# Attention with a learned position bias and a mixture-of-experts layer: half of the last 64 queries' bias transfers issued by GpSimd, bias blocks in alternating order, first tokens split later, later tiles' tokens turned between weights

## The chip, the cores and the metric

The kernel runs on one core of a Trainium2 chip. The metric is the device time of one execution in microseconds (us), as the median of the runs. Engines: TensorE (PE in the profile; PEld is its weight load), VectorE (DVE), ScalarE (ACT), GpSimd (POOL) and SyncE (SP), which here only issues transfers. "L414" is line 414 of the kernel before.

## What is computed

```
scores = q @ k^T / 8                      # 8 batches, 8 heads, 576 queries, head size 64
x      = log1p(|i - j|) / log1p(max(i, 1))
bias   = relu(x * w1 + b1) @ w2           # 32 hidden units, one bias per head, query and key
attn   = softmax(scores + bias) @ v       # the same bias table for all batches
tokens = attn, 4608 rows of 512
logits = tokens @ w_gate + modality_bias  # 8 experts
e      = argmax(logits);  g = softmax(logits)[e]
out    = g * (relu(tokens @ w1[e]) @ w2[e])   # 1024 hidden units
```

## The kernel before

**Bias table.** The table is computed once and stays in SBUF: NBm for the first 512 queries, NBr for the last 64. `bias_table` goes through 32 blocks of 16 queries by 8 heads. `bias_hidden` (L180) computes the 32 hidden units for four queries at a time, four times per block: one of the four on ScalarE (L189), three on VectorE (L191). `bias_out` (L194) multiplies by w2 on TensorE, `bias_put` (L208) scales the result out of PSUM into one of eight rotating buffers, and SyncE issues the transfer of the buffer into the table. Block `blk` of the 32 goes to every eighth partition of NBm from `blk % 8` on (L218). The query rows of NBr come in four late blocks, 32 to 35 (`bias_late`, L260); each of these is moved by four smaller transfers into every eighth partition of one half of NBr (L223, `par` picks the half).

**Attention.** Pairs of heads, 32 of them, run as a pipeline of five steps per pair (`ORDER`), one step for each 128 queries and a last one for the remaining 64 queries of both heads. The string gives the order in which each step's operations are written to the engines: S is scores on TensorE (L400) and the sum with the bias and row minimum on VectorE (L414), e and f the exponentials on ScalarE, t and T the transposes of the result, a, A, b and c the products with v (L486), C a small copy on GpSimd (L434), 0 and 1 the split of the next pair's q and k into a high and a low part (ScalarE casts the high part; GpSimd subtracts for the low part, L384). The late bias blocks are hung into the first pair's steps (`LATE`): blocks 32 and 33 are written ahead of step 0, blocks 34 and 35 ahead of step 1. Only the fifth step of a pair (c = 4) reads NBr. The engines work through their own queues in order, so what is written first is done first on each.

**Experts.** After a batch's attention, routing steps rank its tokens and GpSimd scatters the rows by expert into a DRAM table xg (`s_send`, L857 to L868). Then 18 tiles of 256 tokens of one expert each follow. A tile (`tile`) has phase 1 (96 products with w1, L1212), with the splits of the tile's w2 beside it, and phase 2 (48 products with w2, L1229), with the splits of the next tile's w1 beside it: for each weight part, ScalarE casts the high part and VectorE subtracts for the low part (`wsplit`, L1173 and L1174). The tokens of the next tile are prepared by `xprep`: GpSimd copies gates and ids, VectorE turns the tokens (L1194), ScalarE casts the high part (L1195), VectorE subtracts the low part (L1196). `put_rows` scales a result on ScalarE (L1237) and GpSimd scatters it to the output (L1238).

The first five tiles take tokens of the first six batches, so they run while the last batch is still being routed. `moe_first` hands out those routing steps by a string, one entry per call of `beside` (six per tile; X is a step of the chain with the five `s_send`, B one of the other chain). `first_tiles` hangs the preparation of the first tile into the last five attention steps: `xprep(0)` ahead of step 0, the split of the first w1 columns (`wsplit_cols(0)`, L1181 and L1182) ahead of step 3. A read of xg waits for the writes of xg that are written before it, and the other way round.

Of the kernel before, what the change touches and what calls it, by code (L numbers as in the profile page):

```python
# [22 lines left out]
S = 576  # L23
# [85 lines left out]
class Attn:  # L109
# [8 lines left out]

    ON_POOL, ON_DVE = (), (1,)


    LAG = 1
    PUT_DVE, ON_ACT2 = (21, 31, 34), ()
    TURN0, SPLIT0, QK1 = (4, 8), (6, 10), (9, 10, 11, 12, 13, 14, 15, 16)
    V0 = (0, 1)
    ROUTE = (6, 7, 8, 15, 16, 18)

    ROUTE_LATE = ((1, 1), (1, 2), (1, 3), (1, 4), (2, 0), (2, 1), (2, 3), (3, 0), (3, 1))  # L130

    LATE_HIDDEN = ((31, 0),)
    LATE = ((0, 1), (0, 0), (0, 2), (0, 1), (0, 3), (1, 2), (1, 3))

    def bias_setup(self):
# [72 lines left out]
    def bias_put(self, blk, parts):  # L208
        nc = self.nc
        o = next(self.bias_outs)  # L210
        for cols, ps in parts:
            if blk in self.PUT_DVE:
                nc.vector.tensor_scalar_mul(o[:, cols], ps, self.rpsi[:, blk : blk + 1])
            else:
                nc.scalar.activation(o[:, cols], ps, AF.Copy, scale=self.rpsi[:, blk : blk + 1])
        if blk < NMAIN:
            c, k = divmod(blk, GS)
            nc.sync.dma_start(self.NBm[k:P:GS, H * c : H * c + H, :], o)  # L218
        else:
            for par in range(2):  # L220
                for a in range(2):
                    r = 64 * par + 2 * (blk - NMAIN) + a
                    nc.sync.dma_start(self.NBr[r : 64 * par + 64 : GS, :, :], o[64 * a + par : 64 * a + 64 : 2, :])  # L223

    def bias_table(self, hooks):

        ready = {}
        self.late = [self.bias_late(blk) for blk in range(NMAIN, NBLK)]

        def ahead(blk, cg):  # L230
            if blk < NMAIN and (blk, cg) not in ready:
                by = "pool" if cg == 3 and blk in self.ON_POOL else "act" if cg == 0 and blk not in self.ON_DVE or cg == 1 and blk in self.ON_ACT2 else "dve"
                ready[blk, cg] = self.bias_hidden(blk, cg, by)

        with self.tc.tile_pool(name="bps", bufs=3, space=PSUM) as pp:
            done = []
            for blk in range(NMAIN):
                ps = pp.tile([P, 1024], F32, tag="bps", name=f"bps{blk}")
                if blk + 3 in self.ON_POOL:
                    ahead(blk + 3, 3)  # L240
                for k in range(2):
                    if blk + k not in self.ON_DVE:
                        ahead(blk + k, 0)
                    if blk + k in self.ON_ACT2:
                        ahead(blk + k, 1)
# [3 lines left out]
                for at, k in self.LATE_HIDDEN:  # L249
                    if at == blk:  # L250
                        next(self.late[k])
# [3 lines left out]
                for f in hooks.get(blk, ()):  # L255
                    f()
            for d in done:
                self.bias_put(*d)

    def bias_late(self, blk):  # L260

        hs = [self.bias_hidden(blk, cg, "act" if cg == 0 else "dve") for cg in range(4)]
        yield
        ps = (self.eps[blk % 2].rearrange("p a w -> p (a w)"), self.xbank()[:, 0 : S - 512])
        for cg in range(4):
            self.bias_out(cg, hs[cg], ps)
        self.bias_put(blk, [(slice(0, 512), ps[0]), (slice(512, S), ps[1])])
# [913 lines left out]
        self.nc.scalar.copy(h, w)  # L1181
        self.nc.vector.tensor_tensor(l, w, h.bitcast(F32), op=ALU.subtract)  # L1182

    def xprep(self, t, x):

        nc = self.nc
        gx = self.gx[t % 2]
        for w in range(2):
            at = NDC * TS + 2 * w
            nc.gpsimd.tensor_copy(self.gate(t)[w], gx[:, at : at + 1])  # L1190
            nc.gpsimd.tensor_copy(self.ids_of(t)[w], gx[:, at + 1 : at + 2])
        xh, xl = self.xh[t % 2], self.xl[t % 2]
        x = x.rearrange("p (c w) -> p c w", c=NDC)
        nc.vector.transpose(x, gx[:, 0 : NDC * TS].rearrange("p (a c i) -> p c a i", c=NDC, i=32))  # L1194
        nc.scalar.copy(xh, x)  # L1195
        nc.vector.tensor_tensor(xl, x, xh.bitcast(F32), op=ALU.subtract)  # L1196

    def phase1(self, t, before, beside):
        nc = self.nc
# [47 lines left out]
    def tile(self, t, beside=None, between=()):  # L1247
# [23 lines left out]
        self.load_new(t + 1, 1)  # L1271
        for c in range(NDC):
            self.wsplit(0, c)

        def middle(w):
            if w == 0 and t + 1 < self.T:
                self.xprep(t + 1, self.xt)
            beside()

        self.phase2(t, middle)  # L1280
        if t + 2 <= self.K:
            self.moe_rows(t + 2)
        if t + 2 <= self.T:
# [2 lines left out]
    def first_tiles(self):  # L1286
# [41 lines left out]
    def moe_rest(self, st):  # L1328
# [7 lines left out]
        if K == 0:  # L1336
            self.moe_load(0)
            self.load_new(0, 1)
            self.xprep(0, self.xt)
            self.moe_load(1)  # L1340
        first = self.sure - 2 * NT
        for t in range(K, self.sure):
# [150 lines left out]
```

## Time and profile before

| | |
|---|---|
| three runs | 1004.68, 1006.54 (median), 1007.92 us |
| profiled execution | 1007.5 us, span on the core 1005.4 us |
| busy, PE / DVE / ACT / POOL | 972.1 / 709.4 / 712.7 / 303.1 us |
| mean granted TensorE clock | 0.995 |
| time in the table of biases and the first pair | the first 80 us of the span |
| 32 pairs of attention | until about 573 us |
| 18 tiles | until about 998 us |

The span is what the profiler saw on the core; the execution's own time includes 2.1 us around it. A row of the timeline gives start, duration, engine, line, operation, output and inputs, and in brackets how long the engine had been idle and what ended that. A releaser is inferred: where an instruction waits for several things, the one named is the one that came last by the profile.

### The profile page before, as it was taken

Reading aid. Unit: us, or ns where it says so; the run is one execution under the profiler, and the core shown is the slowest. Engines: PE = TensorE matmul, PEld = TensorE weight load, DVE = VectorE, ACT = ScalarE, POOL = GpSimd, SP = SyncE. Lnnn points to the kernel's source line nnn. Section 1 sums busy time; section 2 is a strip of 40 time slices with the busy share of each in tenths; the row PEclk is TensorE's granted clock in tenths of the full one; section 3 lists DMA queues with packets and bytes.
Section 4 is the critical chain, followed back from the end, with each engine's and each line's share of the span. In section 5 each row is a group of like instructions: output and inputs, shape, how many; then the busy total and the mean of one; then the engine's idle time right before and its main releaser. Section 6 shows DMA issues by size and latency. Waiting matters only on the chain. (4 is left out here: it accounts for less than half of the span.)

```text
span 1005.4 us, 22478 instructions
## 1 busy us (share of the span) xinstructions
PE 972.1 (97%) x8110; PEld 762.4 (76%) x8110; DVE 709.4 (71%) x1441; ACT 712.7 (71%) x1366; POOL 303.1 (30%) x489
## 2 busy tenths in 40 slices
PE   7969999999999999999999899999999999999997
PEld 4547767767677676776667589889999998989896
DVE  8965768776777777777877677886666656565655
ACT  7977988888888888888888555455555555454554
POOL 1512433625426254262542513511111111111111
PEclk9998999999999999999999999999999999999999
DMA  6977755564655646546469430312117821162610
GB/s 163 194 166 152 196 104 116 109 131 101 128 108 105 134 100 120 119 101 133 94 121 212 128 112 32 96 48 64 43 43 190 271 64 54 61 195 68 186 43 24
DMA packets 327417, 116.34 MB, mean 116 GB/s; under 512 B 283247, under 2 KB 304111, under 8 KB 327299
## 3 DMA queue, kind: packets, MB, share of 16 engines
q1 hardware_dynamic: 321234, 95.80, 43.3%
q0 software_dynamic: 5920, 19.03, 5.4%
q8 instruction: 65, 1.06, 0.5%
q14 instruction: 54, 0.43, 0.2%
q10 hardware_dynamic: 144, 0.00, 0.0%
HBM read 144.34 MB, written 33.34 MB: 177 GB/s over the span
## 5 line engine op out<-in xcount | busy, mean ns | idle before, releaser
L414 DVE CUSTOM_DVE_ANT_0 Eb<-sps,NBm 128x576 f32<-128x576 f32 x256 | 183.6, 754 | 125.0 <-PE sps L400 57.1
L429 ACT ACTIVATE Eb<-Eb,mn 128x576 f32<-128x576 f32 x288 | 221.0, 769 | 13.6 <-DVE mn L414 12.6
L332 ACT ACTIVATE eT<-eps 128x512 f32<-128x512 f32 x256 | 148.9, 595 | 55.7 <-PE eps L444 54.8
L400 PE MATMUL sps<-QK 64*128 64x288 f32 (+1 forms) x1728 | 171.7, 310 | 7.5 <-DVE mn L414 7.0
L400 PEld LDWEIGHTS sps<-QK 64*128 64x128 f32 (+1 forms) x1728 | 134.3, 186 | 48.1 <-DVE mn L414 29.6
L1212 PE MATMUL p<-QK,w1hi 128*128 128x256 f32 x1136 | 161.8, 285 | 2.8 <-DVE QK L1196 2.2
L444 PE MATMUL eps<-idf,Eb 128*128 128x128 f32 x1024 | 149.6, 280 | 3.6 <-DVE eT L334 1.9
L1212 PEld LDWEIGHTS p<-QK,w1hi 128*128 128x128 f32 x1136 | 147.1, 191 | 7.3 <-DVE QK L1196 3.0
L486 PE MATMUL xps<-eT,vraw 128*64 128x288 f32 x1024 | 149.3, 416 | 0.0
L444 PEld LDWEIGHTS eps<-idf,Eb 128*128 128x128 f32 x1024 | 113.3, 141 | 37.5 <-issue 13.6
L1238 POOL DMA_INDIRECT out<-mo,idt x36 | 39.5, 1099 | 308.1 <-ACT mo L1237 252.4
L1214 ACT ACTIVATE hh<-p 128x512 fp32r<-128x512 f32 x72 | 43.1, 598 | 123.0 <-PE p L1212 116.7
L1215 DVE SCALAR_TENSOR_TENSOR hl<-p,hh 128x512 fp32r<-128x512 f32 x72 | 49.7, 691 | 101.6 <-ACT hh L1214 97.8
L1229 PE MATMUL p<-w2hi,hh 128*128 128x512 f32 x288 | 112.3, 390 | 0.0
L1229 PE MATMUL p<-w2hi,hl 128*128 128x512 f32 x288 | 112.3, 390 | 0.0
L434 POOL COPY rem<-Eb 128x128 f32<-128x128 f32 x128 | 37.0, 291 | 244.1 <-ACT Eb L429 238.3
L1174 DVE TENSOR_TENSOR w2lo<-NBm,w2hi 128x1024 fp32r<-128x1024 f32 x72 | 89.5, 1243 | 16.0 <-ACT w2hi L1173 15.7
L486 PEld LDWEIGHTS xps<-eT,vraw 128*64 128x64 f32 x1024 | 62.3, 136 | 39.9 <-issue 12.4
L1212 PE MATMUL p<-QK,w1lo 128*128 128x256 f32 x568 | 91.2, 283 | 0.0
L1174 DVE TENSOR_TENSOR w1lo<-NBm,w1hi 128x1024 fp32r<-128x1024 f32 x72 | 85.0, 1243 | 0.0
L1212 PEld LDWEIGHTS p<-QK,w1lo 128*128 128x128 f32 x568 | 78.3, 192 | 0.0
L1173 ACT CAST w2hi<-NBm 128x1024 fp32r<-128x1024 f32 x72 | 74.9, 1040 | 0.0
(219 smaller groups left out, 1451.0 us busy)
## 6 DMA issues: line engine op xcount, KB each, us to landing
NBm<-moe_w SPq DMA_DIRECT2D x84, 512.0 KB
NBm<-moe_w SPq DMA_DIRECT2D x42, 1024.0 KB
NBr<-xg SPq DMA_DIRECT2D x80, 128.0 KB
kraw<-k SPq DMA_DIRECT2D x128, 72.0 KB
xd<-xt SPq DMA_DIRECT2D x128, 72.0 KB
vraw<-v SPq DMA_DIRECT2D x64, 128.0 KB
NBm<-xTb SPq DMA_DIRECT2D x24, 288.0 KB
NBm<-moe_w SPq DMA_DIRECT2D x3, 2048.0 KB
```

The lines of the kernel that those rows point to most:

```text
L332: self.nc.scalar.activation(out, ps, AF.Copy, scale=scale)
L400: nc.tensor.matmul(self.sps[h][:, half, 0:HS], QK[o, q, qs], QK[o, k, HS * half : HS * half + HS], start=i == 0, stop=i == 2, skip_group_c ...
L414: nc.vector.tensor_tensor_reduce(out=e.rearrange("p (t w) -> p t w", t=2), in0=self.sps[h][:, :, 0:HS], in1=nb.rearrange("p (t w) -> p t w ...
L429: self.nc.scalar.activation(e, e, AF.Exp, bias=mn, scale=-1.0, accum_out=sm)
L444: nc.tensor.transpose(ps[:, k, :], e[:, part, P * k : P * k + P], self.idf)
L486: nc.tensor.matmul(ps[out : out + 64, :], lhsT, rhs, tile_position=(row, out), skip_group_check=True, **kw)
L1173: self.nc.scalar.copy(h, w)
L1174: self.nc.vector.tensor_tensor(l, w, h.bitcast(F32), op=ALU.subtract)
L1212: nc.tensor.matmul(ps[:, a, :], w[:, c, fs], x[:, c, :], start=i == 0, stop=i == len(ops) - 1)
L1214: nc.scalar.activation(hh[:, sl, :], ps, AF.Relu)
L1215: nc.vector.scalar_tensor_tensor(hl[:, sl, :], ps, 0.0, hh[:, sl, :].bitcast(F32), op0=ALU.max, op1=ALU.subtract)
L1229: nc.tensor.matmul(ps, h[:, f, sl], m[:, f, :], start=i == 0, stop=i == len(ops) - 1)
```

## The change

The blocks of the bias table are computed in the order 0, 4, 1, 5, 2, 6, 3, 7 within each eight, and the late blocks as 32, 34, 33, 35 (the numbers of the blocks that are put by VectorE, or whose hidden units are all VectorE's, are changed so that the same places in the order are meant). Of the four transfers of a late block, the two into the upper half (`par` 1) are issued by GpSimd. `xprep` is divided into `xturn` (copies and turn) and `xsplit` (cast and subtract). For the first tile the turn stays ahead of step 0, the split moves to step 2, and the split of the first w1 columns from step 3 to step 2. In every tile, the turn of the next tile's tokens moves from the middle of phase 2 in between the second and the third w1 part, and their split behind the fourth part, ahead of phase 2. In the routing string the first `s_send` moves from the last call of tile 1 to the first call of tile 2, and the fifth to the first call in phase 2 of tile 2.

```diff
-    ON_POOL, ON_DVE = (), (1,)
+    SEQ = (0, 4, 1, 5, 2, 6, 3, 7, 8, 12, 9, 13, ...)
+    ON_DVE = (4,)
-    PUT_DVE, ON_ACT2 = (21, 31, 34), ()
+    PUT_DVE = (22, 31, 33)
...
-                    nc.sync.dma_start(self.NBr[r : 64 * par + 64 : GS, :, :], o[64 * a + par : 64 * a + 64 : 2, :])
+                    (nc.sync, nc.gpsimd)[par].dma_start(self.NBr[r : 64 * par + 64 : GS, :, :], o[64 * a + par : 64 * a + 64 : 2, :])
...
-        self.late = [self.bias_late(blk) for blk in range(NMAIN, NBLK)]
+        self.late = [self.bias_late(blk) for blk in (32, 34, 33, 35)]
...
-            for blk in range(NMAIN):
+            for at, blk in enumerate(self.SEQ):
...
-        ps = (self.eps[blk % 2].rearrange("p a w -> p (a w)"), self.xbank()[:, 0 : S - 512])
+        ps = (self.eps[blk // 2 % 2].rearrange("p a w -> p (a w)"), self.xbank()[:, 0 : S - 512])
...
-    def xprep(self, t, x):
+    def xturn(self, t, x):
...
         nc.vector.transpose(x, gx[:, 0 : NDC * TS].rearrange("p (a c i) -> p c a i", c=NDC, i=32))
-        nc.scalar.copy(xh, x)
-        nc.vector.tensor_tensor(xl, x, xh.bitcast(F32), op=ALU.subtract)
+        return x
+
+    def xsplit(self, t, x):
+
+        xh, xl = self.xh[t % 2], self.xl[t % 2]
+        self.nc.scalar.copy(xh, x)
+        self.nc.vector.tensor_tensor(xl, x, xh.bitcast(F32), op=ALU.subtract)
...
         for c in range(NDC):
             self.wsplit(0, c)
-
-        def middle(w):
-            if w == 0 and t + 1 < self.T:
-                self.xprep(t + 1, self.xt)
-            beside()
-
-        self.phase2(t, middle)
+            if c == 1 and t + 1 < self.T:
+                x = self.xturn(t + 1, self.xt)
+        if t + 1 < self.T:
+            self.xsplit(t + 1, x)
+        self.phase2(t, lambda w: beside())
...
-        add(4, 0, lambda: self.xprep(0, self.Eb[:, next(self.e_next)].rearrange("p h s -> p (h s)")[:, 0 : NDC * TS]))
-        add(4, 3, lambda: self.wsplit_cols(0))
+        x0 = []
+        add(4, 0, lambda: x0.append(self.xturn(0, self.Eb[:, next(self.e_next)].rearrange("p h s -> p (h s)")[:, 0 : NDC * TS])))
+        add(4, 2, lambda: self.xsplit(0, x0[0]))
+        add(4, 2, lambda: self.wsplit_cols(0))
...
-        steps = iter("B,X,X,X,,X,BB,,X,B,B,X,X,X,X,X,BB,BB,B,B,B,B,BB,B".split(","))
+        steps = iter("B,X,X,X,,X,BB,,X,B,B,,X,X,X,X,XBB,BB,B,B,B,B,BB,B".split(","))
```

GpSimd at the start of attention, first as it was and then as it is (QK_77 is the next pair's split q and k, rem the small copies; line numbers in the changed kernel are 5 lower there):

```order
L384 TENSOR_TENSOR QK_76<-kT,QK_76 128x576
L434 COPY rem_0_780<-Eb 128x128
L434 COPY rem_1_844<-Eb 128x128
L384 TENSOR_TENSOR QK_77<-qT,QK_77 128x640
L434 COPY rem_2_877<-Eb 128x128
L384 TENSOR_TENSOR QK_77<-kT,QK_77 128x576
L434 COPY rem_3_909<-Eb 128x128
```

```order
L379 TENSOR_TENSOR QK_76<-kT,QK_76 128x576
L223 DMA NBr<-xTb_101 8x4x576 x4
L429 COPY rem_0_780<-Eb 128x128
L223 DMA NBr<-xTb_101 8x4x576 x4
L429 COPY rem_1_844<-Eb 128x128
L379 TENSOR_TENSOR QK_77<-qT,QK_77 128x640
L429 COPY rem_2_877<-Eb 128x128
L379 TENSOR_TENSOR QK_77<-kT,QK_77 128x576
L429 COPY rem_3_909<-Eb 128x128
```

Eight transfers now stand on GpSimd's queue ahead of the two subtractions that make the next pair's low parts; SyncE's run of sixteen becomes one of eight, with everything behind it unchanged.

ScalarE in the last five attention steps, before and changed (QK_76 takes the first tile's tokens, QK_77 the first w1 columns; eT, rT and xTb are the evictions that TensorE's next products wait for):

```order
L429 ACTIVATE Eb,sums_7327<-Eb,mn_4_0_7494 128x576
L1195 CAST QK_76<-Eb 128x1024
L332 ACTIVATE eT<-eps_719 128x4x128
L332 ACTIVATE rT<-xps_82 128x512
L332 ACTIVATE eT<-eps_720 128x4x128
L332 ACTIVATE eT<-eps_719 128x4x2x64
L332 ACTIVATE rT<-eps_720 128x64
L332 ACTIVATE xTb_101<-xps_81 128x288
L1181 CAST QK_77<-NBm 128x1024
```

```order
L424 ACTIVATE Eb,sums_7327<-Eb,mn_4_0_7494 128x576
L327 ACTIVATE eT<-eps_719 128x4x128
L327 ACTIVATE rT<-xps_82 128x512
L327 ACTIVATE eT<-eps_720 128x4x128
L327 ACTIVATE eT<-eps_719 128x4x2x64
L327 ACTIVATE rT<-eps_720 128x64
L1194 CAST QK_76<-Eb 128x1024
L1176 CAST QK_77<-NBm 128x1024
L327 ACTIVATE xTb_101<-xps_81 128x288
```

Both casts now stand between the last rT and the xTb eviction. VectorE's order there is the same as before.

VectorE in phase 2 of the first tile, before and changed (w1lo are the low parts of the next tile's w1, the turn writes xt, QK_77 takes the low part of the tokens):

```order
L800 TENSOR_REDUCE lgs_7778<-lw_7737 128x40
L1174 TENSOR_TENSOR w1lo<-NBm,w1hi 128x1024 x4
L1194 STREAM_TRANSPOSE xt<-NBr 128x1024
L1196 TENSOR_TENSOR QK_77<-xt,QK_77 128x1024
L1215 SCALAR_TENSOR_TENSOR hl<-p_7618,hh 128x512
```

```order
L795 TENSOR_REDUCE lgs_7778<-lw_7737 128x40
L1169 TENSOR_TENSOR w1lo<-NBm,w1hi 128x1024 x2
L1188 STREAM_TRANSPOSE xt<-NBr 128x1024
L1169 TENSOR_TENSOR w1lo<-NBm,w1hi 128x1024 x2
L1195 TENSOR_TENSOR QK_77<-xt,QK_77 128x1024
L1214 SCALAR_TENSOR_TENSOR hl<-p_7618,hh 128x512
```

The same six pieces of work, with the turn two weight parts earlier.

## Rows read from the trace of the kernel before

**Rows 1.** Windows: busy us (instructions) of each engine, PEclk, DMA share, GB/s.

```profile
40.00:60.00 20.00, 18.38 (x222) 9.49 (x218) 19.41 (x50) 16.48 (x28) 0.16 (x1) 1.00 1.05 213
...
65.00:70.00 5.00, 4.00 (x34) 3.35 (x33) 2.97 (x8) 5.00 (x12) 2.84 (x4) 1.00 0.37 109
...
75.00:80.00 5.00, 5.00 (x30) 4.39 (x27) 1.44 (x4) 2.96 (x9) 0.00 (x0) 0.50 0.71 120
...
90.00:95.00 5.00, 4.99 (x45) 4.22 (x43) 4.16 (x10) 4.38 (x10) 0.57 (x2) 1.00 1.01 345
```

**Rows 2.** Timeline of PE, first pairs: start, duration, work, [idle <-releaser].

```profile
67.86 1.05 PE L400 MATMUL sps<-QK 128*128 128x288 f32 x6
...
74.50 1.81 PE L400 MATMUL sps<-QK 64*128 64x288 f32 x12 [4.58 <-DVE mn L414]
...
90.03 1.03 PE L400 MATMUL sps<-QK 128*128 128x288 f32 x6
...
92.12 1.06 PE L400 MATMUL sps<-QK 64*128 64x288 f32 x12
...
104.98 1.05 PE L400 MATMUL sps<-QK 128*128 128x288 f32 x6
```

**Rows 3.** Timeline of DVE, the first instruction that reads NBr.

```profile
73.68 0.76 DVE L414 CUSTOM_DVE_ANT_0 Eb<-sps,NBr 128x576 f32<-128x576 f32 x1 [4.78 <-DMA vraw<-v]
```

**Rows 4.** Line L223: durations in ns min/median/max, first and last start.

```profile
L223 SPq DMA_DIRECT2D NBr<-xTb x16: 588/588/698, 57.5 to 70.6; - x16
```

**Rows 5.** Timeline of POOL, bias table and first pair.

```profile
24.81 15.35 POOL L384 TENSOR_TENSOR QK<-kT,QK 128x576 fp32r<-128x576 f32 x1 [3.84 <-ACT QK L383]
...
60.78 0.29 POOL L434 COPY rem<-Eb 128x128 f32<-128x128 f32 x1 [20.62 <-ACT Eb L429]
...
64.26 1.56 POOL L384 TENSOR_TENSOR QK<-qT,QK 128x640 fp32r<-128x640 f32 x1 [0.34 <-ACT QK L383]
...
67.60 1.44 POOL L384 TENSOR_TENSOR QK<-kT,QK 128x576 fp32r<-128x576 f32 x1 [0.77 <-ACT QK L383]
```

**Rows 6.** Line L868, GpSimd's scattering transfers: durations in ns; time to landing.

```profile
L868 POOL DMA_INDIRECT xg<-xrk,pos x14: 947/986/1025, 190.2 to 572.0; - x14
...
DMA to landing us min/median/max: 2.6/3.5/5.2
```

**Rows 7.** Timeline of DVE and PE, end of the main bias blocks.

```profile
53.51 0.82 DVE L213 TENSOR_SCALAR xt<-bps,xrb 128x576 f32<-128x576 f32 x1 [0.58 <-DMA NBm<-xt]
...
57.87 0.51 DVE L191 TENSOR_SCALAR eT<-xTb,xrb 128x576 f32<-128x576 f32 x1
...
54.47 1.09 PE L199 MATMUL eps<-eT,xrb 128*32 128x512 f32 x8 [1.62 <-DVE taken L916]
```

**Rows 8.** Timeline of ACT, PE and DVE, end of attention.

```profile
562.80 1.04 ACT L1195 CAST QK<-Eb 128x1024 fp32r<-128x1024 f32 x1 [0.48 <-DVE Eb L1194]
...
564.40 0.66 PE L450 MATMUL eps<-idf,Eb 128*128 128x128 f32 x4 [1.24 <-ACT eT L332]
...
569.32 2.33 DVE L1182 TENSOR_TENSOR QK<-NBm,QK 128x1024 fp32r<-128x1024 f32 x1 [3.22 <-ACT QK L1181]
...
572.64 1.04 PE L758 MATMUL xps<-xTb,wgb 128*32 128x512 f32 x2 [1.65 <-DVE xTb L334]
```

**Rows 9.** Waits of PE, 555 us to the end: total us, times, longest.

```profile
PE p L1212 <- DVE QK L1196: 2.2, 4, 1.1
...
PE p L1212 <- ACT QK L1195: 0.7, 2, 0.5
```

**Rows 10.** Timeline of DVE, tokens' low part for tiles 3 and 4.

```profile
643.93 1.76 DVE L1196 TENSOR_TENSOR QK<-xt,QK 128x1024 fp32r<-128x1024 f32 x1 [1.11 <-ACT QK L1195]
...
668.12 1.23 DVE L1196 TENSOR_TENSOR QK<-xt,QK 128x1024 fp32r<-128x1024 f32 x1 [1.12 <-ACT QK L1195]
```

**Rows 11.** Waits of SP's queue (575 to 680 us); timeline of POOL, second row sent.

```profile
SPq L1126 <- DMA xg<-NBm,pos: 14.7, 1, 14.7
...
634.06 1.03 POOL L868 DMA_INDIRECT xg<-NBm,pos  x1 [5.80 <-DMA NBm<-moe_w]
```

More of the change, by code (lines that the diff above doesn't have):

```diff
@@ L117, in __init__ @@
         self.held, self.waiting, self.defer = None, [], 0
-    ON_POOL, ON_DVE = (), (1,)
+    SEQ = (0, 4, 1, 5, 2, 6, 3, 7, 8, 12, 9, 13, 10, 14, 11, 15, 16, 20, 17, 21, 18, 22, 19, 23, 24, 28, 25, 29, 26, 30, 27, 31)
+    ON_DVE = (4,)
     LAG = 1
-    PUT_DVE, ON_ACT2 = (21, 31, 34), ()
+    PUT_DVE = (22, 31, 33)
     TURN0, SPLIT0, QK1 = (4, 8), (6, 10), (9, 10, 11, 12, 13, 14, 15, 16)
@@ L130 @@
     ROUTE_LATE = ((1, 1), (1, 2), (1, 3), (1, 4), (2, 0), (2, 1), (2, 3), (3, 0), (3, 1))
-    LATE_HIDDEN = ((31, 0),)
     LATE = ((0, 1), (0, 0), (0, 2), (0, 1), (0, 3), (1, 2), (1, 3))
@@ L222, in bias_put @@
                     r = 64 * par + 2 * (blk - NMAIN) + a
-                    nc.sync.dma_start(self.NBr[r : 64 * par + 64 : GS, :, :], o[64 * a + par : 64 * a + 64 : 2, :])
+                    (nc.sync, nc.gpsimd)[par].dma_start(self.NBr[r : 64 * par + 64 : GS, :, :], o[64 * a + par : 64 * a + 64 : 2, :])
     def bias_table(self, hooks):
         ready = {}
-        self.late = [self.bias_late(blk) for blk in range(NMAIN, NBLK)]
+        self.late = [self.bias_late(blk) for blk in (32, 34, 33, 35)]
         def ahead(blk, cg):
             if blk < NMAIN and (blk, cg) not in ready:
-                by = "pool" if cg == 3 and blk in self.ON_POOL else "act" if cg == 0 and blk not in self.ON_DVE or cg == 1 and blk in self.ON_ACT2 else "dve"
+                by = "act" if cg == 0 and blk not in self.ON_DVE else "dve"
                 ready[blk, cg] = self.bias_hidden(blk, cg, by)
@@ L236, in bias_table @@
             done = []
-            for blk in range(NMAIN):
+            for at, blk in enumerate(self.SEQ):
                 ps = pp.tile([P, 1024], F32, tag="bps", name=f"bps{blk}")
[L239 to L245, printed above, removed]
+                for b in self.SEQ[at : at + 2]:
+                    if b not in self.ON_DVE:
+                        ahead(b, 0)
                 for cg in range(4):
@@ L248, in bias_table @@
                     self.bias_out(cg, ready.pop((blk, cg)), (ps[:, 0:512], ps[:, 512:S]))
-                for at, k in self.LATE_HIDDEN:
-                    if at == blk:
-                        next(self.late[k])
+                if at == NMAIN - 1:
+                    next(self.late[0])
                 if len(done) == self.LAG:
@@ L254, in bias_table @@
                 done.append((blk, [(slice(0, S), ps[:, 0:S])]))
-                for f in hooks.get(blk, ()):
+                for f in hooks.get(at, ()):
                     f()
@@ L1191, in xprep @@
             nc.gpsimd.tensor_copy(self.ids_of(t)[w], gx[:, at + 1 : at + 2])
-        xh, xl = self.xh[t % 2], self.xl[t % 2]
         x = x.rearrange("p (c w) -> p c w", c=NDC)
         nc.vector.transpose(x, gx[:, 0 : NDC * TS].rearrange("p (a c i) -> p c a i", c=NDC, i=32))
-        nc.scalar.copy(xh, x)
-        nc.vector.tensor_tensor(xl, x, xh.bitcast(F32), op=ALU.subtract)
+        return x
[3 more added lines that the diff above has]
+        self.nc.vector.tensor_tensor(xl, x, xh.bitcast(F32), op=ALU.subtract)
     def phase1(self, t, before, beside):
@@ L1338, in moe_rest @@
             self.load_new(0, 1)
-            self.xprep(0, self.xt)
+            self.xsplit(0, self.xturn(0, self.xt))
             self.moe_load(1)
```

## The prediction

> **What bounds the kernel now.** I read the windows first, because the shares of the whole span (TensorE 97% busy) say little about a change that touches four short stretches. In the long stages TensorE is the bound and has work without a gap. What can be won is its idle time, and the time in which it ran at half clock. The waits of TensorE and then the timeline show where that lies.
>
> *First pair.* The fifth score group of the first pair starts at 67.86, the next pair's first group only at 74.50; one pair later the same two starts are 90.03 and 92.12 [rows 2]. So 6.64 against 2.09: 4.55 us of waiting. TensorE was held by VectorE, and VectorE by its first instruction that reads NBr, which began at 73.68 after 4.78 us of idling [rows 3]. The releaser named there, a load of v, is not read by it; the last of SyncE's sixteen transfers into NBr was issued at 70.6 [rows 4], and it is those that it waited for, 3.1 us after the last issue. The issue is the limit: sixteen starts in 13.1 us, 0.873 us apart [rows 4], while the DMA share is 0.37 [rows 1]. [...] From 74.50 to the next fifth group takes 15.53 us, from 92.12 to the following one 12.86 [rows 2]: 2.67 us more for the same work. Together the pause cost 7.2 us.
>
> *End of the main bias blocks.* VectorE's last result waited 0.58 us for its buffer, held by an earlier transfer, and TensorE started the late blocks right behind it [rows 7].
>
> *End of attention.* TensorE idles 1.24 us behind ScalarE's evictions, and 1.65 us behind VectorE's [rows 8].
>
> *First tiles.* TensorE waits for the next tile's tokens, 2.2 us on the low part and 0.7 on the high part [rows 9].
>
> **The change, part by part, on the scale of the trace before.**
>
> *A. Transfers into NBr.* SyncE keeps eight: from 57.5 at 0.873 us apart the last is issued at 63.6 and, 3.1 us later as now, landed at 66.7 [rows 3, 4]. What stands behind them in SyncE's queue (v, then later q and k) moves up by 7 us, as the pause does. GpSimd gets the other eight. No row shows a plain transfer issued there. The nearest are its scattering transfers of 64 rows, 0.95 to 1.03 us each with a landing 2.6 to 3.5 us after the start, at most 5.2 [rows 6]. From below the bound is SyncE's 0.59 us [rows 4]; from above I take 1.6 us, the longest of GpSimd's plain instructions among VectorE's score work [rows 5]. These transfers have 32 rows, so I take 0.95. VectorE's last hidden units run to 58.38 [rows 7], and GpSimd made no headway beside that kind of work earlier: 15.35 us for a subtraction that takes 1.44 elsewhere [rows 5]. So I start the eight at 58.4: 8 x 0.95 = 7.6 us and the copy of 0.29 in between give 66.3. The last one, started at 65.3, lands between 67.9 and 68.8, at worst at 70.5. VectorE could use it at 68.9, when the fifth group has been computed (67.86 + 1.05) [rows 2]. Wait left: 0 to 1.6 us; I take 0.3.
>
> What is late next is GpSimd's own queue. Behind the eight stand a copy, a subtraction of 1.56, a copy, and the subtraction of 1.44 for the next pair's k [rows 5]: 66.3 + 0.29 + 1.56 + 0.29 + 1.44 = 69.9, against 69.04 before. TensorE's next group would start at 67.86 + 2.09 = 69.95 and needs that low part for its third term. It just fits. With TensorE's pause gone I expect its clock to stay at 1.00, as it is in 65 to 70 with 4.0 of 5 us busy [rows 1]. Gain 7.2 - 0.3 = **6.9 us**; with the bounds, 0 to 7.2.
>
> *B. Order of the blocks.* While the blocks go out the DMA share is 1.05 at 213 GB/s; at 90 to 95 us the same engines move 345 GB/s at 1.01 [rows 1]. So they are held up by something other than the sum of bytes. VectorE is busy 19.41 of those 20 us [rows 1], so faster transfers shorten this stage only where it waits for a buffer: 0.58 us [rows 7], or nothing if the order doesn't matter. I take **0.5**, near the upper end because 345 GB/s shows the room.
>
> [...]
>
> *C. First tile's split.* The token cast of 1.04 us, with 0.48 us of waiting for the turn, stood ahead of the eviction for which TensorE idled 1.24 [rows 8]. It moves behind; that idle goes, 1.2 us. The subtraction for the w1 columns ran from 569.32 to 571.65 in front of the last evictions, after VectorE had idled 3.22 us for a cast that stood behind another eviction [rows 8]. Both casts now run before that eviction, so both subtractions (1.2 us alone, 2.3 as here beside GpSimd's row scaling) fit into those idle 3.22 us and the 1.65 us of TensorE shrink to between 0.1 and 1.65; I take 0.3. The xTb eviction now stands behind two casts; nothing needs it before the logits. Gain 1.2 + 1.35, about **2.6 us**; bounds 0 and 2.9.
>
> *D. Tiles' tokens.* The low part always waited 1.1 us on the cast right behind the turn [rows 10]. With the turn two weight parts earlier the cast runs beside the third and fourth subtraction, so the low part is ready 1.1 us sooner. Of the six waits, 2.9 us in all, the longest are 1.1 and 0.5 [rows 9], so little of them can be left. There the moved routing step helps: SyncE stood 14.7 us until the first row block had been sent, and GpSimd's second row block then idled 5.80 us [rows 11]; whatever is named there, it writes xg and waits for the reads of xg that SyncE could issue only then. That put its scaling beside VectorE's subtraction, 1.76 instead of 1.23 us [rows 10]. With the first send behind that read both waits go. Gain **2.5 us**; bounds 1.2 and 2.9. The result of phase 2's first half is scaled about 2.5 us later on ScalarE, behind the cast; its PSUM tile is one of three, so nobody waits. From the fifth tile on the same move brings and costs nothing, as TensorE hides both orders.
>
> Sum: 6.9 + 0.5 + 2.6 + 2.5 = 12.5 us off the profiled execution's 1007.5 gives **995.0 us**. That execution was 1.0 us above the median of the runs shown; against the median the sum would give 994.0. A difference below 0.3%, 3 us, can't be told from none here.
>
> **The rivals.**
>
> *GpSimd's queue or the landing is late.* At 1.2 to 1.5 us per transfer the next pair's low part comes 2 to 4.4 us later than in A, or the slowest landing of 5.2 us decides: TensorE pauses 2 to 4.5 us at the same place, and a shorter pause can still cost the clock. A falls to between 0 and 4; time 998 to 1002. For it: the fit in A has 0.1 us of room. Against it: scattering 64 rows takes 0.95 us. Chance 0.2.
>
> *The transfers are starved.* If each of GpSimd's transfers is stretched by VectorE's score work, at d us each the low part of k is late by 8 x (d - 0.95). Gain and loss cancel over the whole kernel when that wait reaches 4.55 + 5.6 = 10.2 us (the old wait and the gains of B, C and D), at d = 2.2; at d = 3 the wait is 16.4 us, the pause 11.9 us longer than before, and the time is 1007.5 + 11.9 - 5.6 = 1014. For it: the 15.35 us subtraction [rows 5]. Against it: beside the score work the same subtractions took 1.56 and 1.44 [rows 5]. Chance 0.04.
>
> [...]
>
> *The edits in the tiles don't pay.* If the end of attention and the first tiles are bound by something that merely ends just before (weights' casts, routing on VectorE), C and D bring 1 to 2 us instead of 5.1: about 998.5. For it: for tile 3 VectorE's subtraction took 1.76 us, so others slow it there [rows 10]. Against it: the waits named end on exactly the instructions that move [rows 8, 9]. Chance 0.13.
>
> **How the numbers follow.** The forecast has a chance of 0.63, the rivals 0.2, 0.04 and 0.13. All upper bounds together, 7.2 + 0.6 + 2.9 + 2.9 = 13.6 us, give 993.9; the median lay 1.0 us under the profiled execution and single runs 2 us under the median, and both taken off put the low end near 991; I say 990. The first rival's 1002 is the high end; beyond it lies the starved case and part of the first rival. Faster by over 0.3% is below 1003.5: all but the starved case and some of the first rival, 0.91. Within 0.3%: 0.05. Slower: 0.04.
>
> **What would show it.** A: VectorE's first NBr instruction starts within 2 us of the fifth score group's start, its idle below 1 us, no 0.50 in the clock column around 75 us, and GpSimd's eight transfers near 0.95 us each. B: no wait for a buffer in front of the last main block's result, and a DMA share clearly below 1 at the same GB/s. C: TensorE's idles of 1.24 and 1.65 us gone. D: no wait of L1212 on the tokens. If the pause in the first pair stays above 3 us, or GpSimd's transfers are above 1.5 us, the prediction is wrong in its largest term.

## The result and the profile after

The changed kernel takes 993.56 us (median of five runs, 992.98 to 995.20) against 1007.58 for the kernel before in the same comparison (1004.68 to 1008.15): ratio 0.9872, 95% interval 0.9857 to 0.9886. The forecast was 995.0, worked out for the profiled execution, and the range 990 to 1002. The profiled execution took 995.04 us with a span of 993.2 and a mean granted clock of 0.998; before it was 1007.5, 1005.4 and 0.995. The ratios in this document are not quotients of the two medians, which would be 0.9861 here.

I cut both spans at the same events: the start of the fifth score group of the first pair, that of the second pair, the first expert product, the end of the last product, the end of the span.

| stage, us | before | after | difference |
|---|---|---|---|
| to the first pair's fifth score group | 67.86 | 67.62 | -0.24 |
| from there to the second pair's | 22.17 | 16.16 | -6.01 |
| to the first expert product | 483.59 | 480.65 | -2.94 |
| tiles, to the end of the last product | 424.51 | 420.46 | -4.05 |
| behind the last product | 7.27 | 8.31 | +1.04 |
| sum | 1005.4 | 993.2 | -12.2 |

*First pair.* The windows of the changed kernel (as in [rows 1]):

```profile
40.00:60.00 20.00, 19.00 (x226) 10.26 (x225) 19.99 (x51) 16.60 (x29) 3.18 (x5) 1.00 1.01 226
60.00:65.00 5.00, 3.70 (x35) 2.71 (x33) 4.10 (x12) 4.37 (x11) 3.65 (x7) 1.00 0.94 193
65.00:70.00 5.00, 3.91 (x33) 3.28 (x33) 2.73 (x6) 5.00 (x13) 2.57 (x4) 1.00 0.77 180
...
75.00:80.00 5.00, 5.00 (x52) 3.07 (x52) 3.29 (x8) 4.46 (x13) 1.78 (x4) 1.00 0.68 123
```

The clock column stays at 1.00 where it was 0.50. Between 65 and 70 us the DMA share is 0.77, not 0.37: SyncE's queue has 0.71 of the 0.77 and issues loads of v, q and k from 65.8 on, where before it issued nine of the NBr transfers in these 5 us. The timeline of PE, answering to [rows 2]:

```profile
67.62 1.03 PE L395 MATMUL sps<-QK 128*128 128x288 f32 x6
70.92 1.07 PE L395 MATMUL sps<-QK 64*128 64x288 f32 x12 [1.24 <-DVE mn L409]
...
83.78 1.05 PE L395 MATMUL sps<-QK 128*128 128x288 f32 x6
```

TensorE's pause is 1.24 us in place of 4.58. The timeline of DVE, answering to [rows 3]:

```profile
70.09 0.76 DVE L409 CUSTOM_DVE_ANT_0 Eb<-sps,NBr 128x576 f32<-128x576 f32 x1 [1.43 <-DMA vraw<-v]
```

VectorE's other input, the fifth group's scores, was there at 68.65 (67.62 + 1.03), so NBr still comes last, 4.9 us after SyncE's last start; the load of v that is named as the releaser is not read here. Line L223 (durations in ns, first and last start, count), where GpSimd's share has a row of its own:

```profile
L223 POOL DMA_DIRECT2D NBr<-xTb x8: 541/541/1005, 56.8 to 62.4; - x8
L223 SPq DMA_DIRECT2D NBr<-xTb x8: 588/589/671, 57.5 to 65.2; - x8
...
DMA to landing us min/median/max: 5.1/5.4/7.9
```

A transfer costs GpSimd 0.54 us, the first of them 1.00, but lands 5.1 to 7.9 us after its start. SyncE's eight start 1.10 us apart (7.7 us for seven intervals), wider than the 0.873 of before. The waits of SyncE's queue between 56 and 67 us (us in all, times, longest):

```profile
SPq L223 <- DMA NBm<-xTb: 2.5, 4, 0.8
SPq L223 <- DMA NBm<-xt: 1.4, 2, 0.8
```

So 3.9 us of those starts went into waiting until main blocks had landed; in the kernel before it was 4.1 us (3.1 and 1.0).

*End of attention.* Waits of PE in 545 to 580 us: the 1.24 and 1.65 of [rows 8] are gone, and this one, which was there before, is the only one listed:

```profile
PE eps L439 <- ACT eT L327: 0.7, 1, 0.7
```

Timeline of DVE: both subtractions now stand together behind its idle time, ahead of the last evictions, at 1.22 us each; before, the one for the w1 columns stood there alone and took 2.33.

```profile
560.01 1.22 DVE L1195 TENSOR_TENSOR QK<-Eb,QK 128x1024 fp32r<-128x1024 f32 x1 [3.44 <-ACT QK L1194]
561.16 1.22 DVE L1177 TENSOR_TENSOR QK<-NBm,QK 128x1024 fp32r<-128x1024 f32 x1
```

*Tiles.* Waits of PE from 573 us to the end. Only one of the small products at the end is listed; no wait on tokens (against [rows 9]):

```profile
PE p L1409 <- DVE ht L1402: 0.6, 3, 0.2
```

*End.* The timelines of POOL and ACT at the last two output transfers, of the kernel before:

```profile
994.32 1.13 POOL L1238 DMA_INDIRECT out<-mo,idt  x1 [15.98 <-ACT mo L1237]
...
998.31 0.69 ACT L1237 ACTIVATE mo<-p,gates 128x512 f32<-128x512 f32 x1 [1.47 <-PEq L1354]
999.76 0.98 POOL L1238 DMA_INDIRECT out<-mo,idt  x1 [3.77 <-ACT mo L1237]
```

And of the changed kernel:

```profile
982.96 1.51 POOL L1237 DMA_INDIRECT out<-mo,idt  x1 [13.52 <-issue]
985.06 0.69 ACT L1236 ACTIVATE mo<-p,gates 128x512 f32<-128x512 f32 x1 [3.15 <-PEq L1353]
987.54 0.98 POOL L1237 DMA_INDIRECT out<-mo,idt  x1 [3.06 <-DMA out<-mo,idt]
```

The last transfer started 0.76 us after its scaling ended; now that takes 1.79 us, and what it waits for is the transfer before it. That is the one stage in which the change loses.

### The profile page after: what moved, and what is told of

Its sections match the earlier page's. It is cut to its first block, busy times and chain, and to the rows that moved or that the text cites. A ratio compares the mean times of both kernels' runs of the same rounds, so it can differ in the third digit from the quotient of the medians.

```text
span 993.2 us, 22468 instructions
## 1 busy us (share of the span) xinstructions
PE 968.3 (97%) x8110; PEld 760.0 (77%) x8110; DVE 704.7 (71%) x1441; ACT 710.2 (72%) x1366; POOL 319.0 (32%) x497
## 3 DMA queue, kind: packets, MB, share of 16 engines
q8 instruction: 65, 1.06, 0.5%
## 4 chain that ended last, share of the span: by engine, by line
PE 78%; DVE 7%; ACT 4%; issue 3%; DMA 1%; SPq 0%; POOL 0%; DVEq 0%; POOLq 0%; ACTq 0%
PE p L1211 19%; PE p L1228 16%; PE sps L395 13%; PE xps L481 13%; PE eps L439 10%; ACT Eb L424 2%; ACT eT L327 2%; PE eps L445 1%; DVE Eb L409 1%; PE xps L467 1%; DVE xTb L329 1%; DVE w1lo L1169 1%; PE xps L753 1%; DVE w2lo L1169 1%; PE xps L784 1%
## 5 line engine op out<-in xcount | busy, mean ns | idle before, releaser
L1237 POOL DMA_INDIRECT out<-mo,idt x36 | 47.0, 1307 | 256.7 <-ACT mo L1236 169.4
L481 PEld LDWEIGHTS xps<-eT,vraw 128*64 128x64 f32 x1024 | 62.3, 136 | 40.0 <-issue 12.6
```

The lines of the kernel that those rows point to most:

```text
L481: nc.tensor.matmul(ps[out : out + 64, :], lhsT, rhs, tile_position=(row, out), skip_group_check=True, **kw)
L1237: nc.gpsimd.indirect_dma_start(out=self.out, out_offset=IndirectOffsetOnAxis(ap=ids, axis=0), in_=o, in_offset=None, bounds_check=self.n_t ...
```

## The experiments

Twelve runs; two of them are further profiled executions of the first kernel in the table. Ratios are against the kernel before on the same chip (medians 1006.3 to 1006.9); the stages are from one profiled execution each. "End" is the stage behind the last product.

| kernel | median us | ratio, 95% interval | fifth group to fifth group | five tiles' excess | end |
|---|---|---|---|---|---|
| NBr on GpSimd alone | 1004.36 | 0.9980, 0.9970 to 0.9991 | 17.80 | 5.80 | 6.95 |
| block order alone | 1002.81 | 0.9965, 0.9954 to 0.9976 | 18.93 | - | 6.91 |
| first tile's split alone | 1003.59 | 0.9982, 0.9972 to 0.9991 | 20.89 | - | 7.00 |
| turn and string alone | 1004.06 | 0.9978, 0.9967 to 0.9989 | 22.68 | 2.09 | 8.75 |
| string alone | 1005.58 | 0.9986, 0.9976 to 0.9996 | 20.98 | 4.80 | 7.02 |
| turn alone | 1007.12 | 1.0004, 0.9994 to 1.0014 | 21.24 | 5.13 | 8.97 |
| late blocks' order alone | 1006.58 | 1.0009, 0.9994 to 1.0025 | 22.30 | - | 6.99 |
| all, end mended | 992.31 | 0.9859, 0.9842 to 0.9877 | 15.28 | 1.67 | 7.17 |
| all, 12 of 16 on GpSimd | 998.28 | 0.9922, 0.9897 to 0.9947 | 18.60 | - | 8.81 |
| all, end mended, 4 main blocks on GpSimd | 993.10 | 0.9869, 0.9852 to 0.9886 | 15.41 | - | 7.22 |

"Excess" is what the first five tiles take above 22.42 us each, from the starts of their first products; it was 5.72 before and is 1.65 after. The stretch from fifth group to fifth group varies by itself: in the six profiles in which NBr is sent as before and the main blocks go in the old order it is 20.89 to 22.68, on average 21.7.

**NBr on GpSimd alone.**

```diff
-                    nc.sync.dma_start(self.NBr[r : 64 * par + 64 : GS, :, :], o[64 * a + par : 64 * a + 64 : 2, :])
+                    (nc.sync, nc.gpsimd)[par].dma_start(self.NBr[r : 64 * par + 64 : GS, :, :], o[64 * a + par : 64 * a + 64 : 2, :])
```

> Only the two upper-half transfers of each late block go to GpSimd; order of blocks, tokens and routing as before. Theory 1 (the parts act each at its own place and add up): the start of the fifth score group of the second pair, 90.03 before and 83.78 with the whole change, comes about 5.8 us earlier than before, at 84.2; VectorE's first NBr instruction near 70.3 with an idle of 1.2 to 1.7 us; no stretch at half clock; time 1007.6 - 5.9 = about 1001.7, ratio 0.994. Theory 2 (the alternating order is what lets GpSimd's transfers land in time: in sequential order the backlog of the main blocks holds them up): VectorE's idle ahead of NBr stays at 2.5 us or more, the gain is 4 us or less, time 1003.6 or more.

The time fell by 2.0 us, not 5.9. VectorE's idle ahead of NBr is 3.08 us, so theory 2 holds for the wait. GpSimd's eight transfers landed 6.5 to 8.2 us after their starts, 7.2 at the median, where the changed kernel has 5.4. The timeline of PE in the first profile:

```profile
72.77 1.06 PE L400 MATMUL sps<-QK 64*128 64x288 f32 x12 [2.89 <-DVE mn L414]
...
85.62 1.05 PE L400 MATMUL sps<-QK 128*128 128x288 f32 x6
```

And its window behind the pause:

```profile
75.00:80.00 5.00, 5.00 (x53) 3.12 (x53) 2.64 (x7) 4.99 (x15) 0.51 (x3) 1.00 0.73 135
```

Here the stretch is 17.80 us, a gain of 3.9 against the average of 21.7, about twice what the median of the runs showed. So two more executions were profiled.

> The kernel of a_only, looked at a second time: its ten runs fell in two groups, three at 1002 us with a mean granted clock of 0.997 to 0.999 and seven at 1004.2 to 1005.8 with 0.994 to 0.996; the profile showed one of the first group, with TensorE paused 2.9 us at NBr and no half clock behind it. Theory 1 (the pause, though shorter, costs the clock in most executions): an execution at 1004 us or more shows 0.50 or a value between 0.5 and 0.9 in 70 to 80 us, with 2 to 2.7 us more between the two fifth score groups than the 17.8 of the first look; one at 1002 us shows none. Theory 2 (the two groups differ in how long NBr took to land): the pause itself is 2 us or more longer in a slow execution, at full clock.

> The same as a_only_2, a third look, so that both groups are likely to be seen: the same two theories with the same numbers.

The second profile (1003.39 us) repeats the first at NBr (pause 3.00, stretch 17.92, clock 1.00); its clock falls elsewhere, to 0.67 between 640 and 644 us, behind waits for tokens in the fourth tile. The timeline of PE in the third (1003.94 us):

```profile
73.07 1.07 PE L400 MATMUL sps<-QK 64*128 64x288 f32 x12 [2.91 <-DVE mn L414]
...
87.48 1.03 PE L400 MATMUL sps<-QK 128*128 128x288 f32 x6
```

And the same window there:

```profile
75.00:80.00 5.00, 5.00 (x39) 4.02 (x39) 1.97 (x7) 3.43 (x9) 0.40 (x2) 0.69 0.73 134
```

The same pause, 2.91 against 2.89 us, once with the clock at 1.00 behind it and once at 0.69, and 1.6 us between them in the stretch (19.38 against 17.80). Theory 1 holds in kind, with 1.6 us where it said 2 to 2.7; in the second profile the clock was lost at another place than it said. Theory 2, a longer pause, falls for these three executions; the seven runs at 1004.2 us and above that the two theories were about are not among them.

**Block order alone.**

```diff
-            for blk in range(NMAIN):
+            for at, blk in enumerate(self.SEQ):
...
-        self.late = [self.bias_late(blk) for blk in range(NMAIN, NBLK)]
+        self.late = [self.bias_late(blk) for blk in (32, 34, 33, 35)]
```

> Only the order of the bias blocks is changed; all sixteen NBr transfers stay on SyncE. Theory 1 (the order is worth VectorE's one wait for a buffer): fifth score group of the first pair at 67.62 instead of 67.86, VectorE's NBr instruction still near 73.4 after more than 4 us of idling, the half-clock stretch still there; time 1007.3, not told from no change; in 40 to 60 us the DMA share stays at 1.0 or above and the rate is 210 to 230 GB/s. [...]

It gains 3.5 us, seven times the 0.5 of the forecast. Its window while the main blocks go out:

```profile
40.00:60.00 20.00, 19.00 (x233) 10.28 (x225) 19.99 (x51) 16.60 (x29) 0.85 (x1) 1.00 1.00 234
```

Line L223 there:

```profile
L223 SPq DMA_DIRECT2D NBr<-xTb x16: 588/589/700, 56.8 to 68.6; - x16
```

The first instruction that reads NBr, in the timeline of DVE:

```profile
71.62 0.76 DVE L409 CUSTOM_DVE_ANT_0 Eb<-sps,NBr 128x576 f32<-128x576 f32 x1 [2.65 <-DMA vraw<-v]
```

The rate in 40 to 60 us rose by a tenth (213 to 234 GB/s), and the share was 1.00 against 1.05. Sixteen starts took 11.8 us instead of 13.1, the last was 2.0 us earlier, and VectorE began 2.1 us earlier. Theory 1 is right on the share and wrong on the time: 1002.81 where it had 1007.3. The clock was lost here too: behind a pause of 2.46 us it was 0.80 in 70 to 75 us and 0.86 in 75 to 80.

**Late blocks' order alone.** As above, but the 32 main blocks keep their old order (only the second pair of lines, the late block that VectorE puts, and which PSUM tile a late block uses).

> Against the kernel before only the late blocks' order is changed to 32, 34, 33, 35; the 32 main blocks go out in their old order and all NBr transfers stay on SyncE. Both parts of the new order together moved the last NBr issue from 70.6 to 68.6 and the second pair's fifth score group from 90.03 to 86.86. Theory 1 (the main blocks' order did it: their transfers land sooner, and SyncE's NBr transfers are held by those landings): the last issue stays near 70.6, the group at 89.5 or later, time 1006.5. [...]

Theory 1: nothing gained. The last start is at 71.0 and VectorE's NBr instruction at 74.09, no earlier than before. So the gain comes with the main blocks' order; that order alone was not run, and the late blocks' order may add something once it is there.

**Twelve of sixteen on GpSimd.**

```diff
-                    (nc.sync, nc.gpsimd)[par].dma_start(self.NBr[r : 64 * par + 64 : GS, :, :], o[64 * a + par : 64 * a + 64 : 2, :])
+                    (nc.gpsimd if par or a else nc.sync).dma_start(self.NBr[r : 64 * par + 64 : GS, :, :], o[64 * a + par : 64 * a + 64 : 2, :])
```

> The whole change, with twelve of the sixteen NBr transfers on GpSimd and four on SyncE. Theory 1 (SyncE's half ends last: it still issues its last at 65.2): SyncE is done before 62.5, VectorE's idle ahead of NBr falls from 1.43 us to below 0.7, time 992.8. Theory 2 (the DMA engines are the limit from 57 to 68 us, whoever issues): VectorE's idle stays within 1 us of 1.43, time 993.6. Theory 3 (GpSimd's transfers land late): the last is issued at 65, lands at 71 or later, VectorE's idle is 3 us or more and GpSimd's subtractions are late; time 996 or more.

998.28 us, 4.7 more than the change. Line L223:

```profile
L223 POOL DMA_DIRECT2D NBr<-xTb x12: 541/541/1015, 56.8 to 65.0; - x12
...
L223 SPq DMA_DIRECT2D NBr<-xTb x4: 589/598/671, 56.6 to 61.3; - x4
```

The timeline of PE at the pause:

```profile
71.86 1.69 PE L395 MATMUL sps<-QK 64*128 64x288 f32 x12 [2.15 <-DVE mn L409]
```

The window there:

```profile
70.00:75.00 5.00, 3.14 (x19) 2.87 (x20) 2.05 (x5) 1.63 (x4) 0.00 (x0) 0.70 0.70 125
```

VectorE's idle is 2.35 us, between theories 2 and 3, and behind the pause of 2.15 us the clock came down to 0.70. Three readings matter. SyncE's four starts are 1.57 us apart, but this shows nothing of its queue: each block now has one transfer on SyncE, and the last block's result was there only at 61.28, as ScalarE's timeline shows:

```profile
60.99 0.29 ACT L215 ACTIVATE xTb<-xps,xrb 128x64 f32<-128x64 f32 x1
```

On GpSimd's own queue the ninth transfer was held 1.53 us until an earlier NBr transfer had landed, which put the last start at 65.0:

```profile
63.42 2.15 POOL L223 DMA_DIRECT2D NBr<-xTb  x4 [1.53 <-DMA NBr<-xTb]
```

And SyncE was done with NBr early and issued the loads of v, q and k from 61.95 on, while GpSimd's NBr transfers were still on their way; whether these loads delayed them wasn't tried.

**Four main blocks on GpSimd too** (on the kernel with the end mended).

```diff
-            nc.sync.dma_start(self.NBm[k:P:GS, H * c : H * c + H, :], o)
+            (nc.gpsimd if blk in (26, 30, 27, 31) else nc.sync).dma_start(self.NBm[k:P:GS, H * c : H * c + H, :], o)
```

> The whole change with the end mended as in tail_fix, and the transfers of the last four main blocks (26, 30, 27, 31) issued by GpSimd as well. Theory 1 (SyncE's NBr transfers are held because each waits for an earlier transfer of its own queue to land, the main blocks' being late): SyncE's eight start less than 0.9 us apart instead of 1.10, the last before 64; VectorE's idle ahead of NBr falls from 1.4 to below 0.7, time 991.5. Theory 2 (the bytes in flight are the limit, whoever issues them): VectorE's idle stays between 1 and 2 us, the DMA share in 60 to 65 near 0.94, time 992.3. Theory 3 (GpSimd's transfers are starved beside VectorE's hidden units until 58.4): the four starts take over 2 us each or begin behind 58, NBr's eight are late, VectorE's idle is 3 us or more, time 996 or more.

Line L223:

```profile
L223 SPq DMA_DIRECT2D NBr<-xTb x8: 588/588/670, 56.5 to 62.3; - x8
```

Line L218, two of the four main blocks that GpSimd issues:

```profile
L218 POOL DMA_DIRECT2D NBm<-xTb x2: 562/1724/2887, 50.5 to 53.4; - x2
```

The timeline of DVE at NBr:

```profile
69.28 0.76 DVE L409 CUSTOM_DVE_ANT_0 Eb<-sps,NBr 128x576 f32<-128x576 f32 x1 [0.68 <-DMA kraw<-k]
```

The waits of SyncE's queue between 56 and 67 us:

```profile
SPq L223 <- ACT eT L189: 6.5, 1, 6.5
SPq L223 <- DVE xTb L213: 1.1, 1, 1.1
```

SyncE's eight start 0.83 us apart, the last at 62.3 instead of 65.2: theory 1 on what spaces them. With four main blocks taken off SyncE's queue, the waits for the landing of main blocks (3.9 us in the changed kernel) are gone; the two that are left name engines that make the blocks, not transfers. The time, 993.10, is no better than 992.31: VectorE's idle of 0.68 us was 0.55 in the one profile of the kernel with the end mended, and 1.43 in the change, with the same transfers. What ends that last wait stays open. One of GpSimd's starts, at 50.5, took 2.89 us, and the next, at 53.4, took 0.56, with VectorE busy in 20.00 of the 20 us around them (40 to 60). By the changed kernel's timeline, as an estimate for this one, VectorE works on hidden units until 53.27 and then on a scaling (L213) until 54.02, so the two starts need not have stood beside the same work.

**First tile's split alone** (the diff of `first_tiles` by itself).

> Only the first tile's split and the split of the first w1 columns are moved. Theory 1: the idles of TensorE of 1.24 and 1.65 us at the end of attention go, the distance from the second pair's fifth score group (90.03) to the first expert product (573.62) falls from 483.59 to 480.65, time 1007.6 - 2.9 = 1004.7. Theory 2 (part of it comes from the earlier clock or from the transfers): one of the two idles stays, gain 1.2 to 1.6 us, time 1006.2.

From the second fifth group to the first expert product it takes 480.69 us, as with the whole change (480.65); both idles are gone. Theory 1. By the ratio the time fell by 1.8 us (0.9 to 2.8), by the two medians 2.8. The same stage is 482.6 to 483.6 in the nine profiles without this part, 483.0 on average, and before's was the longest: the part is worth about 2.3 us, and the 2.9 of before against after is partly luck.

**Turn and routing string, together and apart** (the diffs of `tile` and of `steps`).

> Only the tiles' turn and the routing string are changed. Theory 1: no wait of the w1 products on tokens; the distance from the first expert product to the last product falls by 4.0 us, from 424.5 to 420.5, while the end behind the last product grows by 1.0 us, because the last two output transfers now stand closer together and the second waits for the first; time 1007.6 - 3.0 = 1004.6. Theory 2 (the waits sum is all there is): the distance falls by the 2.9 us of listed waits, the end is unchanged, time 1004.7; told apart in the trace only, by 4.0 against 2.9 and by the gap of 1.8 against 0.8 us between the last scaling and the last output transfer.

> Only the routing string is changed; the turn stays in the middle of phase 2, as before. The time of the first five tiles above 22.42 us each was 5.9 us before and 1.7 us with the whole change. Theory 1 (the waits end on the cast right behind the turn, and the string only clears a neighbour out of tile 3's way): the excess falls by 0.5 to 1.1 us, to about 5; tail behind the last product unchanged at 7.0 us; time 1006.4 - 0.8 = 1005.6. Theory 2 (the scattering beside VectorE was the larger part): the excess falls by 2 us or more, time 1004.4 or less.

> Only the tiles' turn and split are moved; the routing string is as before. Theory 1: the excess of the first five tiles falls from 5.9 to about 2.3 us (all but tile 3's interference), the tail grows from 7.0 to 8.3 to 8.8 us, time 1006.4 - 3.6 + 1.5 = 1004.3. Theory 2 (the turn two parts earlier only pays once the string is changed, since VectorE and GpSimd are late in tile 3 otherwise): excess above 3.5 us, time 1005.5.

Excess of the first five tiles, us:

| | 1 | 2 | 3 | 4 | 5 | sum |
|---|---|---|---|---|---|---|
| before | 1.11 | 0.84 | 1.12 | 1.77 | 0.88 | 5.72 |
| string alone | 1.11 | 0.85 | 0.84 | 1.12 | 0.88 | 4.80 |
| turn alone | 1.11 | 0.24 | 0.00 | 3.78 | 0.00 | 5.13 |
| both | 1.11 | 0.24 | 0.00 | 0.13 | 0.61 | 2.09 |

Together 3.6 us, apart 0.9 and 0.6. The times say the same less sharply: by the ratios 2.2 us together, 1.4 for the string, nothing for the turn, and the intervals of the first two overlap. The string alone follows its first theory. The turn takes the waits for tokens out of tiles 2, 3 and 5 and doubles the loss in tile 4, as its second theory said. With the turn alone, the waits of SP's queue (us in all, times, longest):

```profile
SPq L1126 <- DMA xg<-NBm,pos: 17.0, 1, 17.0
```

The timeline of DVE ahead of tile 4:

```profile
634.64 3.46 DVE L1174 TENSOR_TENSOR w1lo<-NBm,w1hi 128x1024 fp32r<-128x1024 f32 x2 [1.73 <-ACT w1hi L1173]
638.02 1.23 DVE L1193 STREAM_TRANSPOSE xt<-NBr 128x1024 f32<-128x1024 f32 x1
639.18 3.12 DVE L1174 TENSOR_TENSOR w1lo<-NBm,w1hi 128x1024 fp32r<-128x1024 f32 x2
```

The timeline of PE in tile 4:

```profile
643.50 0.74 PE L1219 MATMUL p<-QK,w1hi 128*128 128x256 f32 x4 [2.04 <-DVE QK L1200]
```

The window behind that wait:

```profile
644.00:648.00 4.00, 4.00 (x24) 4.00 (x23) 3.48 (x20) 0.51 (x2) 2.32 (x8) 0.57 0.25 73
```

SyncE stands 17.0 us until the first row block is sent, so GpSimd scales the later blocks (1.06 us each, at 634.81 and 639.02) just while VectorE subtracts, and two pairs of subtractions take 3.46 and 3.12 us; with the string changed as well they take 2.35 and 2.31. The low part of the tokens, last in that order, is 2.04 us late, and the clock falls to 0.57 behind it. With both, the tiles took 420.89 us and the last output transfer started 1.93 us behind its scaling: theory 1 of the first text, with 3.6 us gained where it said 4.0 and 1.5 given back at the end where it said 1.0. The end is 8.75 and 8.97 us where the turn is moved, and 7.02 where it isn't.

**End mended.** In the last tile that always runs, the split stands behind the first half's result again:

```diff
-        if t + 1 < self.T:
+        late = t + 1 >= self.sure
+        if t + 1 < self.T and not late:
             self.xsplit(t + 1, x)
...
+            if w == 0 and t + 1 < self.T and late:
+                self.xsplit(t + 1, x)
```

> The whole change, but in the last tile that always runs the split of the next tokens stands behind the first half's result again. Theory 1 (the end grew because ScalarE's cast of the next tokens held back the first half's scaling, and the last output transfer waits for the one before it): the gap between the last scaling's end and the last output transfer falls from 1.8 to 0.8 us, the tail from 8.3 to 7.0 us, time 993.6 - 1.2 = 992.4. Theory 2 (the tail's length is the last transfer's own and varies from run to run): tail stays at 8 us or above, time 993.6.

Timelines of ACT and POOL:

```profile
979.36 0.69 ACT L1236 ACTIVATE mo<-p,gates 128x512 f32<-128x512 f32 x1 [0.28 <-PE p L1228]
...
981.10 1.99 POOL L1237 DMA_INDIRECT out<-mo,idt  x1 [12.94 <-ACT QK L1194]
...
986.27 0.98 POOL L1237 DMA_INDIRECT out<-mo,idt  x1 [3.19 <-ACT mo L1236]
```

The first scaling is at 979.36 instead of 981.23, the last transfer waits for its own scaling again (0.78 us behind it), the end is 7.17 us: theory 1. 992.31 us is below the change's 993.56 by what the end says, though the two intervals overlap; by median it is the fastest of the kernels here.

## Why the prediction was right, and where its steps were not

The sum was 12.5 us against 12.2 in the two profiles. Its terms were less good than the sum, and that they add up to it is partly luck: A and B together gave 6.25 us where 7.4 was forecast, C and D 6.99 where it was 5.1, and the end took back 1.04 that the forecast had at nothing.

*A, 6.9 us: the mechanism was right, the reason for the limit was not.* The step that failed is "the issue is the limit: sixteen starts in 13.1 us, 0.873 us apart". Starts stood 1.10 us apart with eight on SyncE, and 0.83 with eight when four main blocks had left its queue. Of the time between starts, the profiles put 4.1 us before and 3.9 after down to waits until main blocks ahead of them on that queue had landed; with the four blocks gone, none. So SyncE's last start came at 65.2 and not 63.6, its half wasn't landed at 66.7, and VectorE began at 70.09. In the first pair A by itself gave 3.3 us (mean of its three profiles, 18.37, against 21.7), the two orders alone 2.8 in one profile, both 6.0 (mean of 16.16 and 15.28): within what single profiles tell, the two add up there.

Two prices for GpSimd were wrong and cancelled. I took 0.95 us a start, between 0.59 and 1.6: it was 0.54 at the median, below my lower bound, and the first four ran beside VectorE from 56.81 on in 2.66 us, only the first of them stretched (1.00). I took 2.6 to 3.5 us to landing, at worst 5.2: it was 5.1 to 7.9. By the median, as an estimate, the last one, started at 62.4, landed near 67.8, where I had 67.9 to 68.8; by the longest it would be 70.3, so which queue's transfer came last isn't shown. The low part of the next k, with "0.1 us of room" in the forecast, was done at 68.8 instead of 69.9.

*B, 0.5 us: wrong by its place.* The wait for the buffer went, as said. But the step "faster transfers shorten this stage only where it waits for a buffer: 0.58 us" looked at the stage alone. The transfers also stand ahead of NBr, and there the new orders were worth 3.5 us by themselves, the late blocks' order alone nothing. GpSimd's NBr transfers show it as well: with the old order they landed 7.0 to 7.2 us after the start (medians of three profiles), with the new one 5.4 and 4.8 (the change, and the change with the end mended). What I gave to A, all of the pause, belongs in near equal parts to A and B by the first pair's stretch.

The share was to fall clearly below 1 and did not: 1.01 at 226 GB/s, 1.00 at 234 with the order alone, 1.05 at 213 before. In these 20 us the five kernels with the new order moved 226 to 239 GB/s, those with the old one 207 to 214; VectorE, busy in 19.99 of the 20 us in the changed kernel, sets the pace of the stage, so this is not what the transfers could reach. Why the new order moves about a tenth more, no run shows.

*The clock* stayed at 1.00, as forecast. The remark that "a shorter pause can still cost the clock" is shown: at 2.15 us in the kernel with twelve on GpSimd, at 2.46 in the one with the block order alone, and at 2.91 in one of three profiles of A alone. Whether that is why A alone brought only 2.0 us by the median stays open: none of its seven slower runs was profiled, and the block order alone gained 3.5 us although its profile shows the loss.

*C, 2.6 us:* 2.94, or 2.3 against the average of the profiles without it; the mechanism was right, and nothing of the 0.3 that I left was there.

*D, 2.5 us:* 4.05 in the tiles, and 1.04 given back at the end. Two steps failed. The gain was taken from the idle listed for the waits, which was too little: 2.83 us of listed waits on tokens in the first five tiles went, and with them 4.07 us of excess (5.72 to 1.65). The ends of products are modelled in the profile, so part of the difference may lie in how idle is counted; that stays open. And "its PSUM tile is one of three, so nobody waits" looked for the wrong waiter: behind the last tile the output transfers wait. That the string clears the way for the turn was in the forecast as an aside; the run of the turn alone shows that it gains nothing by itself (1007.12 us against 1006.85).

*The rivals.* That GpSimd's queue or the landing is late, at 998 to 1002, came about with twelve transfers on GpSimd: 998.28. There the landing was late, not the low part of the next k, which was done at 69.0 as before. A stretched start shows once, 2.89 us with four main blocks on GpSimd; the one behind it took 0.56, and in the changed kernel the NBr transfers, the first at 56.81 and so ahead of the end of VectorE's hidden units at 58.13, 0.54 us by the median and 1.00 at most. What stretched the one is not shown. The tile edits paid.

## What to carry to other kernels

Where transfers on one queue start wider apart than one costs, look at what lands ahead of them on that queue before dividing them over engines: reordering the earlier transfers and moving half of the later ones were worth about the same in the first pair here (2.8 and 3.3 us). Price a moved step where the engine's work ends as well as in its loop. And try parts of a change apart: one of these, the turn, gains nothing until another one has cleared its place.

## What was not expected of the hardware

A plain transfer of 72 KB cost GpSimd 0.54 us to start, less than SyncE's 0.59, and landed 5.1 to 7.9 us later in the changed kernel, with the transfers of the main blocks still on their way (SyncE's queue waited 3.9 us for them between 56 and 67 us). The ninth such transfer on GpSimd's queue was held 1.53 us until an earlier one had landed (twelve on GpSimd). The same pause of TensorE, 2.89 to 3.00 us, left the clock at 1.00 twice and was followed by 0.69 once; shorter ones, 2.15 and 2.46 us, were followed by 0.70 and 0.80. The fourth tile can lose the clock as well: 0.67 between 640 and 644 us in one profile, behind waits of 0.46 and 1.19 us, and 0.57 between 644 and 648 with the turn alone.
